# w1's last 96 columns computed beside wqkv's third block, the last rows of the second MLP product packed two token tiles at a time, and the order of work taken from a table

## The chip, the cores and the metric

The kernel runs on one core of one Trainium2 chip. The metric is the device time of one execution in microseconds (us). The kernel before takes 415.14 us (median of three executions, 414.89 to 415.17). The execution that the profiler recorded took 415.18 us, of which 413.4 us lie between its first and its last instruction (the span).

## The reference

For 2048 tokens of 512 numbers, two branches share one layer norm, and the first is gated by the second:

```python
xn = layernorm(x)
# A: sliding, dilated attention: 32 heads of 16, each token sees 8 tokens, two apart
qkv = xn @ wqkv                       # 512 x 1536
o = softmax(q . k[idx] / 4) @ v[idx]  # idx = s, s-2, ..., s-14
s = o @ wo                            # 512 x 512
# B: MLP
h = gelu(layernorm(xn) @ w1 + b1)     # 512 x 1376
m = h @ w2 + b2                       # 1376 x 512
out = x + s * silu(m)
```

## The kernel before

All large products run on PE in float16, each operand split into a high and a low half, so one float32 product is three float16 products (high times high, low times high, high times low).

The tokens are split by parity into two sequences (c = 0, 1) of eight tiles of 128 tokens. The kernel runs eight **attention units** u = (c, hb): each takes one block hb of wqkv (128 columns each of q, k and v, 384 in all). In `qkv` every one of the eight token tiles costs 12 products of 384 columns (L746: four slices of 128 input rows, three half pairs), and ACT or DVE writes the result scaled into U[0] or U[1] (L759, L763). `attention` then runs on DVE: four products and four sums for the logits (L805, L808), the softmax, four products with v (L863, L901 in the last unit), and sums on POOL and DVE. A transposing transfer (L851) brings the result into oT.

The **MLP** goes in four chunks of 512 tokens. 1376 = 10 x 128 + 96, so w1 has eleven column blocks f = 0 to 10, the last of 96 columns. `mlp1` makes, for each f, 12 products of 512 columns into a ps bank (L1016); ACT applies the gelu and makes the high half (L1033, L1036), DVE the low half (L1038). `mlp2` multiplies by block f of w2 two steps later, 12 products of 512 columns into four banks z, one per token tile (L1052). The last block has 97 rows there: 96 and one of ones for b2; its tile is `hlast`. After it ACT applies the silu (L1063, L1068). `wo_first` (L929) and `wo_last` (L961) multiply the attention result by wo, and DVE and POOL combine it with the gate and x.

**Order.** Nothing here is scheduled at run time: every engine works off its instructions in the order written. That order is made while the program is built, by a planner (`Plan`): each operation has an engine, a cost, a priority and the operations it waits for, and the planner always takes the one that can start first, by priority among those. All transfers are issued by SP. PE starts with 24 products of constants (L1169) that keep it working, then takes tokens 6 and 7 of sequence 0 in float32 straight from the loaded data (L617).

In the opening (about 0 to 46 us) x, wqkv and w1 are loaded, normed, split and, for four of the eight tiles, transposed on PE (L683) or by a transfer (L675); units 0 and 1 then run their `qkv`.

Of the kernel before, what the change touches and what calls it, by code (L numbers as in the profile page):

```python
# [33 lines left out]
LASTPOOL = (0, 2, 4)  # L34

# [3 lines left out]
LAG = 2  # L39

# [4 lines left out]
BYDMA = (4, 5, 6, 7)  # L45
TRZ = (3, 3, 0, 2, 0, 1, 1, 0)
PTR = (0.5487, 0.3388, 0.0342, 0.6565, 0.7826, 0.1978, 0.0549, 0.9)
GROUPS = ((0,), (1, 2), (3, 4, 5), (6, 7))
BATCHES = ((0, 1, 2, 3, 4, 5), (6, 7))
LOADS = (('t', 6), ('q', 0), ('q', 2), ('x', 2), ('x', 0), ('q', 4), ('t', 7), ('x', 5), ('x', 1), ('x', 3), ('x', 4), ('q', 6), ('w', 0), ('w', 2), ('x', 7), ('c', 2), ('s', 1), ('c', 0), ('w', 3), ('x', 6), ('w', 1), ('c', 1), ('b', 0), ('s', 0))  # L50
HI_ENG = ('act', 'act', 'act', 'dve', 'dve', 'dve', 'dve', 'act')
XT = (0, 4, 30, 34)
Y_ENG = ('pool', 'act', 'dve', 'dve', 'act', 'pool', 'dve', 'act')

W1ENG = ('act', 'dve', 'act', 'act', 'act', 'act', 'act')
# [3 lines left out]
W2LO = ('dve', 'dve', 'dve', 'dve', 'dve', 'pool', 'dve')  # L59
EV0 = ('act', 'dve', 'dve', 'act', 'act', 'act', 'dve', 'dve')  # L60
EV1 = ('dve', 'dve', 'act', 'act', 'act', 'act', 'dve', 'act')
QLO0 = ('pool', 'dve', 'dve', 'pool')
QLO1 = ('dve', 'dve')
W1LO = ('dve', 'dve', 'pool', 'dve', 'dve', 'dve', 'dve')
WOLAG = 2
MEANBY = ('dve', 'pe', 'pool', 'pool')
W2LATE = 6

BEFORE_W1 = (0, 1, 4, 5)

# [26 lines left out]
class Plan:  # L97
# [9 lines left out]
    def add(self, eng, dur, fn, reads=(), writes=(), prio=None, table=None, nbytes=0,  # L107
            after=None, holds=(), port=False, rate=350e3, issue=0.55, tail=1.4):
# [56 lines left out]
    def start(self):  # L165
        for o in self.ops:
            o.npred, o.ready, o.succs = len(o.preds), 0.0, []
        for o in self.ops:
            for p in o.preds:
                p.succs.append(o)  # L170
        self.free = {o.eng: 0.0 for o in self.ops}
        self.portfree, self.dma, self.landed, self.table = 0.0, 0.0, [], None

    def earliest(self, o):
# [3 lines left out]
        if o.eng == "sp" and o.nbytes:  # L178
            left = FLIGHT
            for end, n in reversed(self.landed):  # L180
                left -= n
                if left < 0:
                    t = max(t, end)
                    break
        return t

    def place(self, o, t):

        if o.eng == "sp":
# [3 lines left out]
            self.dma = max(self.dma, t + o.issue + 0.3)  # L193
            self.dma += o.nbytes / (o.rate if self.dma > SLOW else 265e3)
            end = self.dma + o.tail
            self.landed.append((end, o.nbytes))
            return end
        end = t + o.dur
        if o.nbytes:
            self.free[o.eng] = end  # L200
            self.dma = max(self.dma, end + 0.3) + o.nbytes / o.rate
            return self.dma + o.tail
# [19 lines left out]
    def issue(self):  # L222
# [55 lines left out]
SLOW = 5.5  # L278

FLIGHT = 0.9e6  # L280

PW2 = 1.1284
PS2 = 0.4252
PWQ1 = 0.9
PW1 = 0.423
PB1 = 0.75
PCS = 0.6
PQ0 = 0.2677
PSQ0 = 0.1788
PMEAN = 0.04  # L290
PDIR = (0.192, 0.1517, 0.1187, 0.1556)
PG = (0.5671, 0.5205, 0.3952, 0.4033)
PY = (0.8339, 0.1477, 0.3649, 0.4824, 0.05, 0.5767, 0.05, 0.8333)
PU0 = 0.8687
PU1 = 0.969
PWARM = 0.9
PEV = 0.2698

PTOT = 0.5899

WAKE = 24
PS1 = 1.1561
# [3 lines left out]
PQLO = 0.5225  # L306

PFPLN = 0.35
PSEC = (0.6153, 0.7518, 0.1)

U1MH = 4
# [5 lines left out]
IORD0 = (6, 7, 0, 4, 1, 3, 2, 5)  # L317
IORD1 = (7, 0, 6, 3, 2, 4, 5, 1)
MLPN = (7, 7, 6, 4, 7, 7, 2, 0)
# [7 lines left out]
def tile_mixer(ctx, tc, a_x, a_xt, a_wqkv, a_wo, b_w1, b_b1, b_w2, out):  # L327
# [34 lines left out]
    ident = sb.tile([P, P], F32, name="ident")  # L362
    make_identity(nc, ident)
    fours = sb.tile([P, 2 * P], BF16, name="fours")
    nc.vector.memset(fours, 4.0)
    mean1 = sb.tile([P, P], F32, name="mean1")
    nc.vector.memset(mean1, 1.0 / D)
    halves = sb.tile([P, 16], F32, name="halves")
# [3 lines left out]
    misc = sb.tile([P, 512], F32, name="misc")  # L372
    v0 = misc[64:65]


    wq = sb.tile([P, NHB, 2, KT, 384], F16, name="wq")
    w1 = sb.tile([P, 2, KT * F], F16, name="w1")
# [6 lines left out]
    b1T = sb.tile([P, NF], F32, name="b1T")  # L384
    hlast = sb.tile([P, 2, 512], F16, name="hlast")
# [7 lines left out]
    R_mx = Ring(sb, [P, 64], F32, 4, "mx")  # L393
    R_cs = Ring(sb, [P, NI], F32, 8, "cs")
# [72 lines left out]
    def low_pool(n, lo, get, s, hi, **k):  # L467
# [4 lines left out]
        pool(0.45 + n * 3.9e-3, fn, **k)  # L472
# [25 lines left out]
    def k0(hb):  # L498
        return dict(rate=400e3, tail=0.6, issue=0.45) if hb == 0 else dict(tail=3.5) if hb > 1 else {}
# [9 lines left out]
    def scale_q(hb):  # L509
        col = R_s.new()  # L510
        for k in range(0, KT, 2):
            def go(k=k):
                src = stq[hb]()[:, k * 384:(k + 2) * 384]
                nc.scalar.activation(wq[:, hb, 0, k:k + 2].bitcast(BF16),
# [11 lines left out]
    def prep_q(hb):  # L526
# [3 lines left out]
        for k in range(0, KT, st):  # L530
            n = st * 384
            dst = [wq[:, hb, t, k:k + st].rearrange("p k e -> p (k e)") for t in range(2)]
            src = lambda k=k, n=n: stq[hb]()[:, k * 384:k * 384 + n]
# [17 lines left out]
    def factors(n, V, vs, mk, cdst, ckeys):  # L551
# [12 lines left out]
            rb.t[:, 0:n], p0b.t[:, 0:n], halves[:, 0:n], op=ALU.pow), [p0b], [(rb, 0)], port=False)  # L564
        with pl.fuse():
# [5 lines left out]
            cdst, a1(), halves[:, 8:8 + n], op=ALU.pow), [(A, 1)], ckeys, port=False)  # L571
# [53 lines left out]
    def ln0(g):  # L625
        q, n = cpos[g[0]], len(g)
        for i in g:
# [8 lines left out]
            rb0[:, q:q + n], pb0[:, q:q + n], halves[:, 0:n], op=ALU.pow), [("pb", g)], [("rb", g)], port=False)  # L636

    def second(g):
# [4 lines left out]
        with pl.fuse():  # L643
# [5 lines left out]
            cT[:, 0, q:q + n], x1, halves[:, 8:8 + n], op=ALU.pow), [("ab", g)], [("c", 0, i) for i in g], port=False)  # L649

    def y0(i):
# [12 lines left out]
        elif Y_ENG[i] == "pool":  # L664
            pool(1.25, lambda: nc.gpsimd.tensor_scalar(x(), x(), mv0[:, q, 0:1], rb0[:, q:q + 1], op0=ALU.subtract,
# [701 lines left out]
```

## Time and profile before

| | |
|---|---|
| time, median of three | 415.14 us |
| profiled execution, its time | 415.18 us |
| its span | 413.4 us |
| ACT busy | 222.1 us (54%) |
| POOL busy | 120.3 us (29%) |
| products with wqkv, L746 | 744 |
| first product of the MLP, L1016 | 528 |
| second product of the MLP, L1052 | 528, 48 of them with `hlast` |

A row of the profile gives busy time, the mean of one instruction in ns and the idle time of its engine just ahead. PE products overlap: the recorded length of one product is longer than the distance from one start to the next, and a stream of them costs the distance. In a timeline a row is a group of like instructions, with its start, its length and their count. SPq is the queue in which SP issues transfers.

### The profile page before, as it was taken

How to read it: one execution, taken by the hardware profiler on the slowest of the kernel's cores; microseconds unless marked ns; L12 is line 12 of the kernel's file. 1: busy time of each engine (PE TensorE's matmuls, PEld its weight loads, DVE VectorE, ACT ScalarE, POOL GpSimd, SP SyncE). 2: the span in 40 equal slices, each digit the busy share in tenths (PEclk: the TensorE clock that was granted, in tenths of full speed). 3: DMA queues.
4: the chain of work that ended last, by engine and by line, in shares of the span. 5: the costliest groups of instructions: out<-in, count | busy, mean ns of one | idle time of the engine just before them, and what ended most of it. 6: DMA issues, size and time to landing. Idle time of an engine off the chain costs nothing.

```text
span 413.4 us, 5554 instructions
## 1 busy us (share of the span) xinstructions
PE 405.9 (98%) x2083; PEld 206.6 (50%) x2083; DVE 379.5 (92%) x379; ACT 222.1 (54%) x353; POOL 120.3 (29%) x131
## 2 busy tenths in 40 slices
PE   8799999999999999999999999999999999999996
PEld 5555544445654455445544554455455544444443
DVE  4996989998999999989998999999999998999954
ACT  4699899994549655843384252225212393263500
POOL 3834002004380425042504330434033404520021
PEclk9999999999999999999999999999999999999999
DMA  8958717030045137720172034223604244007133
GB/s 281 397 112 258 235 61 230 0 128 1 1 142 152 28 93 183 149 46 2 48 221 75 0 102 116 68 86 88 205 7 122 88 111 145 0 18 238 23 102 131
DMA packets 47211, 46.41 MB, mean 112 GB/s; under 512 B 31785, under 2 KB 32225, under 8 KB 46673
## 3 DMA queue, kind: packets, MB, share of 16 engines
q1 hardware_dynamic: 47184, 46.06, 37.6%
q8 instruction: 16, 0.26, 0.3%
q14 instruction: 11, 0.08, 0.1%
HBM read 24.06 MB, written 7.34 MB: 76 GB/s over the span
## 4 chain that ended last, share of the span: by engine, by line
PE 92%; ACT 3%; issue 1%; DVE 1%; POOL 1%; ACTq 0%
PE z L1052 28%; PE ps L1016 28%; PE ps L746 25%; PE ps L929 5%; PE ps L961 2%; PE z L961 2%; PE pl L746 1%; ACT w L421 1%; PE pl L961 1%; ACT f L673 1%; ACT yT L687 0%; ACT wq L536 0%; POOL wq L471 0%; POOL rb L635 0%; ACT prod L661 0%
## 5 line engine op out<-in xcount | busy, mean ns | idle before, releaser
L1016 PE MATMUL ps<-yT,w 128*128 128x512 f16 (+1 forms) x528 | 120.4, 379 | 0.0
L746 PE MATMUL ps<-wq,yT 128*128 128x384 f16 x708 | 117.0, 326 | 0.2 <-DVE U L759 0.2
L1052 PE MATMUL z<-w,h 128*128 128x512 f16 x480 | 110.4, 379 | 0.0
L746 PEld LDWEIGHTS <-yT 128*128 128x128 f16 x744 | 72.5, 98 | 49.2 <-issue 1.0
L1016 PEld LDWEIGHTS <-w 128*128 128x128 f16 (+1 forms) x528 | 52.8, 100 | 61.0
L805 DVE TENSOR_TENSOR prod<-U 128x2048 f32<-128x2048 f32 x32 | 73.2, 2286 | 2.2 <-POOL prod L883 0.7
L1052 PEld LDWEIGHTS <-h 128*128 128x128 f16 x480 | 46.6, 98 | 55.5 <-issue 0.3
L808 DVE TENSOR_REDUCE L<-prod 128x128 f32<-128x2048 f32 x32 | 73.0, 2281 | 0.4
L1033 ACT ACTIVATE ps<-ps,b1T,hsc 128x512 f32<-128x512 f32 (+1 forms) x44 | 32.9, 748 | 73.4 <-PE ps L1016 72.2
L863 DVE TENSOR_TENSOR prod<-pl,U 128x2048 f32<-128x2048 f32 x28 | 63.2, 2283 | 4.2 <-POOL prod L873 4.1
L763 ACT ACTIVATE U<-ps,cs 128x384 f32<-128x384 f32 x54 | 31.2, 580 | 65.2 <-PE ps L746 65.2
L873 POOL TENSOR_TENSOR prod<-prod,prod 128x2048 f32<-128x2048 f32 x7 | 31.7, 4531 | 113.8 <-DVE prod L863 99.6
L883 POOL TENSOR_TENSOR prod<-prod 128x1024 f32<-128x1024 f32 x14 | 32.9, 2349 | 0.0
L882 POOL COPY gate<-prod 1x1 f32<-1x1 f32 x21 | 5.5, 264 | 91.0 <-DVE prod L805 82.2
L1038 DVE SCALAR_TENSOR_TENSOR h<-ps,hsc,h 128x512 f16<-128x512 f32 x40 | 29.6, 741 | 1.7 <-ACT h L1036 1.4
L1036 ACT ACTIVATE h<-ps,hsc 128x512 f16<-128x512 f32 x40 | 27.3, 684 | 1.3 <-PE z L1052 0.4
L929 PE MATMUL ps<-wo,oT 128*128 128x512 f16 x96 | 21.7, 379 | 0.0
L858 DVE TENSOR_TENSOR prod<-prod,prod 128x2048 f32<-128x2048 f32 x9 | 20.5, 2282 | 0.0
L1033 ACT ACT_TABLE_LOAD x10 | 12.8, 1283 | 8.6 <-PE ps L1016 8.5
L883 POOL TENSOR_TENSOR prod<-prod,prod 128x1024 f32<-128x1024 f32 x7 | 16.4, 2347 | 0.0
L961 PEld LDWEIGHTS <-oT 128*128 128x128 f16 x108 | 10.6, 98 | 10.4
L929 PEld LDWEIGHTS <-oT 128*128 128x128 f16 x96 | 9.4, 98 | 11.2
(179 smaller groups left out, 377.8 us busy)
## 6 DMA issues: line engine op xcount, KB each, us to landing
f<-in_A_x_dram SPq DMA_DIRECT2D x31, 256.0 KB, 3.5
U<-U SPq DMA_DIRECT2D x16, 392.0 KB, 4.0
gd<-f SPq DMA_DIRECT2D x12, 256.0 KB, 3.4
prod<-in_A_x_dram SPq DMA_DIRECT2D x8, 256.0 KB, 6.9
oT<-in_B_w_dram SPq DMA_DIRECT2D x2, 1024.0 KB
yT<-in_B_w_dram SPq DMA_DIRECT2D x2, 1024.0 KB, 7.9
f<-gd SPq DMA_DIRECT2D x8, 256.0 KB, 2.7
out_dram<-f SPq DMA_DIRECT2D x8, 256.0 KB, 2.8
```

Of the source, the lines that this page charges most:

```text
L746: nc.tensor.matmul(b.t[:, 0:384], y[:, s, k, o:o + P], wq[:, hb, t, k], start=(n == 0), stop=(n == 11))
L763: act(384, lambda i=i, b=b: nc.scalar.activation(U3[:, i:i + 31:15, :], b.t[:, 0:384].rearrange("p (t e) -> p t e", t=3), AF.Identity, sca ...
L805: dve(2048, lambda p2=p2, g=g: nc.vector.tensor_tensor(p2(), q, slots(Ut, KH, 2 * g), op=ALU.mult), qk + [("kh", ub, 0), ("kh", ub, 1), (" ...
L808: dve(2048, lambda pr=pr, g=g: nc.vector.tensor_reduce(L3()[:, 2 * g:2 * g + 2], pr.t.rearrange("p (r f d) -> p r f d", r=2, d=DH), AX.X, ...
L863: dve(2048, lambda: nc.vector.tensor_tensor(pr.t.rearrange("p (r f d) -> p r f d", r=2, d=DH), A3()[:, 2 * g:2 * g + 2].rearrange("p r (f ...
L873: pool(4.75, lambda: nc.gpsimd.tensor_tensor(acc.t, acc.t, p1.t, op=ALU.add), [acc, p1], [acc])
L883: nc.gpsimd.tensor_tensor(x.t[:, 0:1024], x.t[:, 0:1024], y(), op=ALU.add)
L929: nc.tensor.matmul(b.t, oT[:, hb, i // 4, s, i % 4], wo[:, t, hb], start=(hb == 0 and n == 0), stop=(hb == last and n == 2))
L961: nc.tensor.matmul(b.t[:, cols], oT[:, hb, i // 4, s, i % 4], wo[:, t, hb, cols], start=(start and hb == 0 and n == 0), stop=(stop and hb ...
L1016: nc.tensor.matmul(b.t[0:M], w1[:, s, f * 512 + k * M:f * 512 + (k + 1) * M], yT[ch][:, t, k], start=(n == 0), stop=(n == 11))
L1033: act(512, lambda: nc.scalar.activation(b.t[0:M], b.t[0:M], AF.Gelu_apprx_tanh, bias=b1T[0:M, f:f + 1], scale=hsc[0:M, 1:2]), [b, ("b1T",) ...
L1052: nc.tensor.matmul(z.t, hl[s][0:K, t * P:(t + 1) * P], w2[0:K, w, f], start=(f == 0 and n == 0), stop=(f == NF - 1 and n == 2))
```

## The change

**The last 96 columns of w1** are no longer a step of `mlp1`. They lie beside the 384 columns of wqkv's third block (`HLAST = 2`), and `qkv` of that block makes 480 columns per product. The result is now tokens by columns, not columns by tokens. A new function, `last_block`, handles it per chunk of 512 tokens: ACT copies the 96 columns out of the ps bank, POOL adds b1 (loaded as a row on all partitions), ACT applies the gelu and makes the high half, DVE makes the low half in two pieces, and two transposing transfers bring it to columns by tokens.

**The second product** with that block has 3 x 96 + 2 rows to sum. They are packed as two products of 128 rows (96 high rows and 32 low rows each, beside rows of w2 arranged to match) and 34 rows left over. The 34 rows of two token tiles stand on partitions 0 to 33 and 64 to 97 (`hlc`, `w2t`), so the two products of a pair use different rows of the array and different banks. Where there were 12 products per chunk there are now 8 of 128 rows and 4 of 34 rows.

**Around it:** w2 is loaded in two more pieces and split with three more ACT and two more DVE operations; five of seven high halves of w1 are made on DVE (one before); three low halves of w2 are made on POOL (one before); both float32 tiles take their mean from PE; the first row of v goes through DRAM and not through SBUF; other tiles go through the transposing transfer.

**The order** is a table, `ORDER`, with one number per operation. The planner takes the operations in that order and no longer chooses. Its costs for transfers were changed too, but they no longer decide anything.

```diff
+HLAST = 2
-BYDMA = (4, 5, 6, 7)
+BYDMA = (2, 5, 6, 7)
-GROUPS = ((0,), (1, 2), (3, 4, 5), (6, 7))
+GROUPS = ((0,), (1,), (2, 3, 4), (5,), (6, 7))
-W1ENG = ('act', 'dve', 'act', 'act', 'act', 'act', 'act')
+W1ENG = ('dve', 'dve', 'act', 'dve', 'dve', 'act', 'dve')
-MEANBY = ('dve', 'pe', 'pool', 'pool')
+MEANBY = ('pe', 'pe', 'pe', 'dve')
+ORDER = (
+    2, 1, 4, 8, 0, 5, 112, 131, 115, 133, 135, 127, 121, 130, 125, 114, 118, 128, 25, 124, 120, 119, 116, 26,
...
-        order = []
+        order, fixed = [], [self.ops[n] for n in reversed(ORDER)]
         while len(order) < len(self.ops):
             best = None
-            for e, cand in engs.items():
+            if fixed:
+                o = fixed.pop()
...
+                best = (t, o)
+            for e, cand in engs.items() if best is None else ():
...
+    FR = P - FL
+
+    def last_block(ch):
+        n = 4 * FL
+        h16 = R_f.new()
+        v = lambda: h16.t.bitcast(F16).rearrange("p (t a f) -> p t a f", a=2, t=4)
...
+        with prio(PEV):
+            pool(1.0, lambda: nc.gpsimd.tensor_tensor(x3(), x3(), row, op=ALU.add), xk + [("b1T",)], xk)
+            act(n, lambda: nc.scalar.activation(x, x, AF.Gelu_apprx_tanh), xk, xk,
+                aps=1, table="gelu")
+            act(2 * n, lambda: nc.scalar.activation(
+                v()[:, :, :, 0:FL], x.rearrange("p (t o f) -> p t o f", t=4, o=1).to_broadcast([P, 4, 2, FL]),
+                AF.Identity, scale=hsc[:, 2:3]), xk + [("hsc2",)], [(h16, 0)])
...
+            low(lambda: v()[:, :, :, FL:P], 0, 2 * FR, (h16, 1))
+            low(lambda: hrem.rearrange("p a b (o f) -> p (a b) o f", o=2)[:, :, 0:1, 0:FR], 2 * FR, FL, ("hreml",))
...
+            dma(P * 2048, lambda: nc.sync.dma_start_transpose(dst, h16.t.bitcast(F16)), [(h16, k) for k in range(2)] + [("hreml",)],
+                [("hl", ch % 2)], rate=1e6, issue=1.3, tail=0.8)
+            dma(P * 512, lambda: nc.sync.dma_start_transpose(hlc[ch % 2], hrem.rearrange("p a b f -> p (a b f)")),
+                [("hreml",), ("hrem",)], [("hlc", ch % 2)], rate=1e6, issue=1.3, tail=0.8)
...
+        wide = 384 + FL * (hb == HLAST)
...
-                    nc.tensor.matmul(b.t[:, 0:384], y[:, s, k, o:o + P], wq[:, hb, t, k],
+                    nc.tensor.matmul(b.t[:, 0:wide], y[:, s, k, o:o + P], wq[hb][:, t, k],
...
+            if hb == HLAST:
+                act(FL, lambda i=i, b=b: nc.scalar.activation(
+                    hpt[i // 4][:, (i % 4) * FL:(i % 4 + 1) * FL], b.t[:, 384:384 + FL], AF.Identity, scale=hsc[:, 1:2]),
+                    [b, ("hsc",)], [("hp", i // 4, i % 4)], prio=PEV, after=pl.users([("hp", i // 4, i % 4), ("hl", i // 4)]))
+        for j in range(2 if hb == HLAST else 0):
+            last_block(2 * c + j)
...
+        for a in range(0, 4, 2) if f == NF - 1 else ():
+            def pair(a=a, z=list(zt)):
+                ha = hlt[ch % 2].rearrange("p a (t x) -> p (a t) x", t=4)
+                for t in range(a, a + 2):
+                    for w in range(2):
+                        nc.tensor.matmul(z[t].t, ha[:, 2 * t + w], w2[:, w, f], start=False, stop=False)
+                for t in range(a, a + 2):
+                    r = slice(64 * (t - a), 64 * (t - a) + FR + 2)
+                    nc.tensor.matmul(z[t].t, hlc[ch % 2][r, a // 2], w2t[r], start=False, stop=True)
...
-            if p < len(steps):
+            if p < len(steps) and steps[p][1] < NF - 1:
                 with prio(PR_M + p * 10):
                     mlp1(*steps[p])
```

Three places where the order moves. First **SP**, the first loads of the program (U1 takes the float32 tokens and wqkv's second block, prod0 wqkv's first block, prod1 and prod2 the tiles of x). Before:

```order
L1124 DMA U1_87<-in_A_xt_dram 128x512
L505 DMA prod0_93<-in_A_wqkv_dram 128x768 x2
L1099 DMA prod1_94<-in_A_x_dram 128x512 x2
L505 DMA U1_87<-in_A_wqkv_dram 128x768
L1124 DMA U1_87<-in_A_xt_dram 128x512
L1099 DMA prod2_95<-in_A_x_dram 128x512
```

With the change:

```order
L1254 DMA U1_94<-in_A_xt_dram 128x512
L586 DMA prod0_100<-in_A_wqkv_dram 128x768
L1229 DMA prod1_101<-in_A_x_dram 128x512 x2
L1254 DMA U1_94<-in_A_xt_dram 128x512
L1229 DMA prod2_102<-in_A_x_dram 128x512
L586 DMA prod0_100<-in_A_wqkv_dram 128x768
L586 DMA U1_94<-in_A_wqkv_dram 128x768
```

The second half of wqkv's first block moved from third place to seventh, behind three tiles of x and the second float32 tile.

Second **PE**, the second product with the last block, first chunk (z00 to z30 are the banks of the four token tiles; hl0 holds the two packed products, tail the 34 rows). Before, inside the twelve products:

```order
L1052 LDWEIGHTS hlast_91
L1052 MATMUL z00_143<-w2_80,hlast_91 128x512
L1052 LDWEIGHTS hlast_91
L1052 MATMUL z10_144<-w2_80,hlast_91 128x512
L1052 LDWEIGHTS hlast_91
```

With the change:

```order
L1170 LDWEIGHTS hl0_98
L1170 MATMUL z10_148<-w2_87,hl0_98 128x512
L1173 LDWEIGHTS tail_78
L1173 MATMUL z00_147<-tail_78 128x512
L1173 LDWEIGHTS tail_78
L1173 MATMUL z10_148<-tail_78 128x512
L1170 LDWEIGHTS hl0_98
L1170 MATMUL z20_149<-w2_87,hl0_98 128x512
```

Each bank now gets two products of 128 rows, and the 34-row products of two banks follow each other.

Third **ACT**, at the end of unit 2's `qkv` (U0 takes its results; first and hl0 take the 96 columns of chunks 1 and 0). Before:

```order
L1036 ACTIVATE h2_108<-ps2_141,hsc_154 128x512
L763 ACTIVATE U0_86<-ps1_140,cs2_115 128x3x128
L482 ACTIVATE wo_81<-yT2_84,osc_158 128x1024
L763 ACTIVATE U0_86<-ps0_139,cs2_115 128x3x128
L482 ACTIVATE wo_81<-yT2_84,osc_158 128x1024
L763 ACTIVATE U0_86<-ps2_141,cs2_115 128x3x128
```

With the change:

```order
L884 ACTIVATE hl0_98<-ps0_143,hsc_158 128x96
L563 ACTIVATE wo_88<-yT2_91,osc_162 128x1024
L880 ACTIVATE U0_93<-ps1_144,cs2_120 128x3x128
L880 ACTIVATE U0_93<-ps0_143,cs2_120 128x3x128
L880 ACTIVATE U0_93<-ps2_145,cs2_120 128x3x128
L1394 ACTIVATE w2_87<-f6_109,zsc_160 32x512
L884 ACTIVATE first_65<-ps2_145,hsc_158 128x96
L816 ACT_TABLE_LOAD
L816 ACTIVATE hl0_98<-hl0_98 128x384
L818 ACTIVATE f0_103<-hl0_98,hsc_158 128x8x96
```

Between the copy of the last 96 columns and the gelu of chunk 0 stand six operations and a load of ACT's function table; before there was no such chain.

More of the change, by code (lines that the diff above doesn't have):

```diff
@@ L107, in add @@
     def add(self, eng, dur, fn, reads=(), writes=(), prio=None, table=None, nbytes=0,
-            after=None, holds=(), port=False, rate=350e3, issue=0.55, tail=1.4):
+            after=None, holds=(), port=False, rate=390e3, issue=0.45, tail=0.8):
         if self.fused is not None and eng == self.fused["eng"]:
@@ L178, in earliest @@
         if o.eng == "sp" and o.nbytes:
[L179 to L184, printed above, removed]
+            if len(self.landed) >= FLIGHT:
+                t = max(t, self.landed[-FLIGHT])
         return t
@@ L383, in tile_mixer @@
     cT = sb.tile([P, DIL, NI], F32, name="cT")
-    b1T = sb.tile([P, NF], F32, name="b1T")
-    hlast = sb.tile([P, 2, 512], F16, name="hlast")
+    b1T = sb.tile([P, NF + FL], F32, name="b1T")
+    hl0 = sb.tile([P, 512], F32, name="hl0")
+    hpt = [hl0[:, 0:512], first[:, 0:512]]
+    hlt = [h.bitcast(F16).rearrange("p (a t) -> p a t", a=2) for h in hpt]
     gd = dr.tile([DIL, NI, P, D], F32, name="gd")
@@ L854, in emit_o @@
                 [(o16, 0, h0), (o16, 1, h0)], [("oT", hb, h) for h in range(h0, h1)] +
-                ([("s1a", n, 0) for n in range(2)] if u == 0 else []), rate=600e3, issue=1.6)
+                ([("s1a", n, 0) for n in range(2)] if u == 0 else []), rate=1e6, issue=1.3 + 0.7 * (h1 - h0 - 1), tail=0.9)
         def add(n, a, b, d, keys, dkey):
```

268 lines of the change are left out of this document (159 added, 109 removed), and 61 rows, old and new, of the table ORDER.

## The prediction

> **What bounds the kernel now.** I read the busy times of the page first, then its chain of waits, then a table of stretches, then the timeline of the opening and of the end.
>
> ```profile
> PE 405.9 (98%) x2083; PEld 206.6 (50%) x2083; DVE 379.5 (92%) x379; ACT 222.1 (54%) x353; POOL 120.3 (29%) x131
> PE 92%; ACT 3%; issue 1%; DVE 1%; POOL 1%; ACTq 0%
> 0.00:12.00 12.00, 9.82 (x44) 6.12 (x44) 6.31 (x19) 6.11 (x11) 5.24 (x14) 1.00 0.85 298
> 12.00:34.00 22.00, 20.38 (x121) 12.29 (x122) 20.80 (x58) 17.77 (x33) 11.05 (x11) 1.00 0.77 239
> 34.00:389.00 355.00, 354.96 (x1814) 177.82 (x1811) 338.62 (x285) 196.36 (x308) 100.24 (x104) 1.00 0.34 98
> 389.00:410.00 21.00, 20.76 (x109) 10.38 (x106) 13.08 (x19) 1.86 (x3) 3.82 (x3) 1.00 0.36 109
> ```
>
> The stretches give PE, PEld, DVE, ACT, POOL, the granted clock and the transfers. From 34 to 389 us PE stands still for 0.04 us of 355, at full clock, and the chain lies on it for 92% of the span. So a product less on PE is time less, as long as nothing takes PE's place. The candidate is DVE: 338.62 of 355 us busy in the same stretch, with 16.4 us to spare. ACT and POOL have 150 us and more.
>
> **The price of a product** comes from the chain, where a piece is a stretch of PE without a gap.
>
> ```profile
> 101.60 15.60 PE ps L746 x96
> 378.65 2.59 PE ps L1016 x12
> 408.45 1.32 PE ps L961 x12
> L1052 PE MATMUL z<-w,hlast 97*128 97x512 f16 x48 | 11.0, 379 | 0.0
> 378.49 2.75 PE L1016 MATMUL ps<-yT,w 128*96 128x512 f16 x12
> 381.08 5.34 PE L1052 MATMUL z<-w,h 128*128 128x512 f16 x24
> 386.26 2.75 PE L1052 MATMUL z<-w,hlast 97*128 97x512 f16 x12
> 388.85 5.99 PE L961 MATMUL ps<-wo,oT 128*128 128x512 f16 x27
> ```
>
> 384 columns cost 15.60/96 = 0.1625 us, 512 cost 2.59/12 = 0.216, 256 cost 1.32/12 = 0.110. That is a straight line of 0.418 ns per column. Narrowness elsewhere buys nothing: the 96-column block takes from 378.49 to 381.08, 2.59 us, and the 97-row product from 386.26 to 388.85, again 2.59 us.
>
> **The change part by part.** *First product, last block:* 4 chunks x 12 products go: -4 x 2.59 = -10.36 us. They come back as 96 more columns in 2 units x 8 tiles x 12 = 192 products. That is 192 x 96 x 0.418 ns = +7.70 us. Net -2.66.
>
> *Second product, last block:* -4 x 2.59 = -10.36 us again. There come 4 x 8 = 32 products of 128 rows, 32 x 0.216 = +6.91 us, and 8 pairs of 34 rows. No row shows two products on different rows of the array. A pair costs at least one product's distance, 0.216 us, which is 8 x 0.216 = 1.73 in all. At most the two run one after the other, and the array empties ahead of the pair and behind it. What emptying costs is in the row of 48: one product is recorded with 379 ns, a stream costs 216 each, so 163 ns of each lie under the next. Then a pair costs 0.432 + 0.326 = 0.758 us, 6.06 in all. I take 0.30 us, which is 0.216 and half of one emptying, since the pair shares neither array rows nor banks: 8 x 0.30 = +2.40. Net 6.91 + 2.40 - 10.36 = -1.05 (from -1.72 to +2.61).
>
> The page TensorEngine Tiling (Array Packing) of the Trainium skill, section Key Properties, speaks against the change here: going over to another tiling mode drains TensorE. By it each pair has two drains, and with 163 ns for one and full overlap between, eight pairs cost 8 x 0.54 = 4.3 us. The second product would then come out 0.9 us dearer than before. The page TensorE: Matmul & The Clock Gate of the Trainium skill, section on packing small matmuls, has tiles start about 4 ns apart. By it alone eight pairs cost 1.8 us. No trace here has yet shown either.
>
> *Opening.* Here the table changes nearly every row, so I walked it with durations of before.
>
> ```profile
> 6.84 0.84 ACT L514 ACTIVATE wq<-prod 128x768 bf16<-128x768 f32 x1 [1.41 <-DMA prod<-in_A_wqkv_dram]
> 8.92 2.13 ACT L536 ACTIVATE wq<-prod,qsc 128x384 f16<-128x384 f32 x4 [1.15 <-DVE qsc L459]
> 9.83 0.97 PEld L599 LDWEIGHTS ps<-U,mean 128*128 128x128 f32 x8 [0.40 <-DMA U<-in_A_xt_dram]
> 15.96 0.81 PE L746 MATMUL ps<-wq,yT 128*128 128x384 f16 x4
> 19.54 4.71 PE L746 MATMUL ps<-wq,yT 128*128 128x384 f16 x28
> 24.44 5.36 PE L746 MATMUL ps<-wq,yT 128*128 128x384 f16 x32 [0.19 <-DVE U L759]
> 41.19 5.20 PE ps L746 x32
> 46.38 10.36 PE ps L1016 x48
> ```
>
> Before, 8 + 28 = 36 products of units 0 and 1 are done by 24.44 us; the other 132 need 132 x 0.1625 = 21.45 us and end at 46.38, so 0.5 us is lost there. Now wqkv's second half of block 0 is the seventh load, with 2048 KB through it. Before, 2176 KB had landed at 9.83, so it lands near 9.5 and not near 6.84 us. ACT then has 14.5 us of rows in series (four squares, four scalings of 0.53 and two of 0.92, four tiles to norm, four casts) ahead of the high half of block 1, which is ready between 23.4 and 24.1 us. PE's order has 36 products of block 0 ahead of it, from about 16.2 us; they end near 23. So PE enters block 1 0.3 to 1.0 us sooner, and loses perhaps the 0.5 us elsewhere. I take -0.6 us. A walk over some forty rows may miss by 2 us each way: -2.5 to +1.5.
>
> *The new chain to the second product* has one narrow place, chunk 0. Its order on PE after unit 2's last product has 36 products of w1 and 12 of w2, 48 x 0.216 = 10.4 us, and then reads the transposed block.
>
> ```profile
> L763 ACT ACTIVATE U<-ps,cs 128x384 f32<-128x384 f32 x54 | 31.2, 580 | 65.2 <-PE ps L746 65.2
> L536 ACT ACTIVATE wq<-yT,qsc 128x768 f16<-128x768 f32 x4 | 3.6, 921 | 0.0
> L1033 ACT ACT_TABLE_LOAD x10 | 12.8, 1283 | 8.6 <-PE ps L1016 8.5
> L863 DVE TENSOR_TENSOR prod<-pl,U 128x2048 f32<-128x2048 f32 x28 | 63.2, 2283 | 4.2 <-POOL prod L873 4.1
> 370.05 2.09 SPq L851 DMA_TRANSPOSE oT<-o  x1
> ```
>
> ACT's last write of the unit (0.58), a w2 scaling (0.7), a copy (0.3), the table load (1.28), the gelu (0.6) and the high half of 768 (0.92) end 4.5 us after the unit. DVE's two small low halves (0.7 together) and the transfer (2.1) make it 7.3. But two products with v of 2.28 stand ahead on DVE, and the second low half and the 34 rows of w2 (three more DVE operations) follow. So it is 9 to 12 us against 10.4. I take +0.3 us (0 to 1.5). The other three chunks have a whole unit or several steps as cover.
>
> *Costed at nothing:* 16 copies, 4 gelus and 4 high halves on ACT (some 11 us, against 9 that go with the block's eight and four high halves of w1), POOL's bias adds and w2 halves (POOL is idle 293 us), two more loads and eight transposes on SP. DVE loses and gains about as much: four low halves of 0.74, the mean of one tile and three halves of weights go, eight small low halves, w1's high halves and two w2 operations come. I make it +0.7 us. All this is hidden by PE's stream, and costs its length if DVE falls behind.
>
> ```profile
> 389.58 0.74 DVE L848 SCALAR_TENSOR_TENSOR o<-prod,osc,o 128x512 f16<-128x512 f32 x1
> 390.34 4.67 SPq L851 DMA_TRANSPOSE oT<-o  x2
> 392.97 0.75 DVE L848 SCALAR_TENSOR_TENSOR o<-prod,osc,o 128x512 f16<-128x512 f32 x1 [0.79 <-ACT o L846]
> 396.62 2.10 PE L961 MATMUL ps<-wo,oT 128*128 128x512 f16 x9
> ```
>
> *The end* shows the cover. The attention's first half is written at 390.3 us and landed 2.1 us later, 392.4; PE asks for it at 396.6, 13.2 us before its last product ends at 409.8. The change puts nine products of other tiles ahead of that, so that PE asks 39 x 0.216 + 24 x 0.11 = 11.1 us before its end. With PE ending 4 us sooner, near 405.7, it asks at 394.6: DVE may come 2.2 us later than before, and 0.7 uses a third of that.
>
> **Sum:** -2.66 - 1.05 - 0.6 + 0.3 = -4.0 us on the profiled 415.18 us (span 413.4 and 1.78 around it), so 411.2. The median of three is 0.04 lower: 411.1 us.
>
> **The rivals.** (a) *Every pair drains the array twice.* 0.54 instead of 0.30 us makes eight pairs 1.9 us dearer, the rest as forecast: 413.0 us. For it: 163 ns do lie under each product. Against: nothing in the trace changes shape, so nothing shows the price. The tiling page of the Trainium skill, cited above, is this rival's rule.
>
> (b) *DVE takes PE's place, at the last attention unit.* The first attention now starts later, since DVE makes four more high halves of w1 ahead of it: 2944 columns at 0.49 us for 512 (row below) are 2.8 us. If DVE keeps its 12 idle us of the middle and adds this, its first half is written more than 2.2 us later and each further us costs one. Slower than before by 0.2% needs 4.0 + 2.2 + 0.8 = 7 us of delay: 416.5 us. For it: DVE has only 16.4 us of slack in 355. Against: it stood idle 3 us between 36 and 40 us, which the earlier work now fills. A smaller delay, 1.5 to 3 us beyond the cover, gives 412.6 to 414.1.
>
> ```profile
> 32.19 0.49 DVE L480 TENSOR_SCALAR w<-oT,hsc 128x512 f16<-128x512 f32 x1
> 36.00:38.00 2.00, 2.00 (x14) 1.22 (x13) 0.34 (x3) 1.97 (x4) 1.97 (x1) 1.00 0.58 210
> 38.00:40.00 2.00, 2.00 (x14) 1.21 (x13) 0.66 (x2) 2.00 (x5) 1.58 (x1) 1.00 0.82 240
> ```
>
> (c) *The table gains more.* Pairs fully side by side (-0.7 more) and a stream that enters block 1 2 us sooner: 408.8 us. For it: PE's idle time, 3.8 us ahead of 34 us, is all in the opening. Against: the walk, where ACT holds block 1 to 23.4 or later.
>
> (d) *The change does not do what it says:* 480 columns cost a whole bank's 0.216 us. Then 192 x 0.0535 = 10.3 us come back and not 7.7: 413.8 us. Against: 256, 384 and 512 lie on one line.
>
> **Chances.** Forecast 0.50 (its own range 409.6 to 412.4), (a) 0.15, (b) 0.17, of which 0.09 slower than before, (c) 0.13, (d) 0.05. A measurement of this kernel tells about 0.2%, 0.83 us, from no change. Faster than 414.3 us are the forecast, (a), (c), most of (d) and the small case of (b): 0.86. Within 0.2% I give 0.05, slower 0.09. The range reaches to (c) below and past (a) and (d) above: 408.7 to 414.0 us.
>
> **What would show it.** Right: groups of 480 columns with 96 in 19.4 us; no row of 96 columns by 512; the 34-row products in starts a few ns apart; PE without gaps after the opening; the first product of the MLP's second stage with the packed block without a wait. Wrong: gaps of over 0.1 us around the 34-row products (a); PE waiting for oT in the last 15 us (b); PE waiting for the transposed block or for DVE after unit 2; more or less than 36 products of wqkv done at 24 us (opening).

## The result, and the profile after

The changed kernel takes **429.74 us** (median of four executions, 427.39 to 430.08) against 415.01 us for the kernel before beside it: 1.0343 times as long, with a 95% interval of 1.0306 to 1.0381. The forecast was 411.1 us, 408.7 to 414.0. It was wrong in sign. The profiled execution took 430.0 us, with a span of 428.2.

The page of the changed kernel answers to the lines shown of before: busy times, the chain of waits by engine, and the granted clock in 40 slices.

```profile
PE 408.4 (95%) x2041; PEld 200.9 (47%) x2041; DVE 391.8 (91%) x388; ACT 223.3 (52%) x372; POOL 128.8 (30%) x139
PE 74%; DVE 10%; issue 5%; DMA 3%; POOL 2%; ACT 2%; SPq 1%; DVEq 0%; POOLq 0%; ACTq 0%
PEclk9999999999998999999999999999999999989998
```

PE has 42 products fewer and is busy 2.5 us longer. It stands idle for 19.8 us of the span, where it stood 7.5 before, and the chain lies on it for 74% and no longer for 92%. The clock, which was full all through, dips.

The view of what PE waits for names the places (time in total, times, longest):

```profile
PE z L1170 <- DMA hl<-f: 3.4, 1, 3.4
PE ps L1052 <- DVE f L1066: 2.5, 1, 2.5
PE ps L1139 <- DVE h L1157: 2.0, 1, 2.0
PE z L516 <- ACT w L1364: 1.6, 1, 1.6
```

None of these waits was there before. The timeline of PE shows what follows the first three; the start is in front, the wait in brackets:

```profile
131.58 1.86 PE L1170 MATMUL z<-w,hl 128*128 128x512 f16 x4 [3.40 <-DMA hl<-f]
308.79 4.44 PE L1052 MATMUL ps<-wo,oT 128*128 128x512 f16 x12 [2.45 <-DVE f L1066]
377.04 4.44 PE L1139 MATMUL ps<-yT,w 128*128 128x512 f16 x12 [2.00 <-DVE h L1157]
```

Twelve products take 4.44 us here and 2.59 elsewhere; four take 1.86 and not 0.86. The table of stretches shows why (PE, PEld, DVE, ACT, POOL, clock, transfers):

```profile
308.00:310.00 2.00, 1.21 (x4) 0.53 (x4) 2.00 (x4) 0.07 (x1) 1.89 (x2) 0.75 0.00 0
310.00:312.00 2.00, 2.00 (x7) 0.62 (x5) 1.97 (x2) 0.45 (x1) 0.00 (x0) 0.50 0.00 0
312.00:314.00 2.00, 2.00 (x10) 0.90 (x9) 2.00 (x2) 0.24 (x1) 0.00 (x0) 0.89 0.00 0
```

The granted clock falls to one half about when PE starts again, and stays there for 3.4 us: the three stretches lack 0.25, 0.50 and 0.11 of 2 us each, 1.72 us in all.

**Who is late.** DVE's busy time rose from 379.5 to 391.8 us. The timelines of DVE and POOL show four rows with most of it; here are three, with POOL's rows beside them:

```profile
122.44 4.00 DVE L825 SCALAR_TENSOR_TENSOR hrem<-hl,hsc,f 128x128 f16<-128x128 f32 x1 [1.09 <-ACT f L818]
302.97 5.11 DVE L928 TENSOR_TENSOR prod<-U 128x2048 f32<-128x2048 f32 x1 [1.70 <-ACT h L1155]
350.49 6.24 DVE L928 TENSOR_TENSOR prod<-U 128x2048 f32<-128x2048 f32 x1
121.77 4.53 POOL L996 TENSOR_TENSOR prod<-prod,prod 128x2048 f32<-128x2048 f32 x1
301.42 4.51 POOL L996 TENSOR_TENSOR prod<-prod,prod 128x2048 f32<-128x2048 f32 x1 [12.49 <-DVE prod L986]
305.89 3.05 POOL L815 TENSOR_TENSOR first<-first,b1T 128x384 f32<-128x384 f32 x1
350.06 4.51 POOL L996 TENSOR_TENSOR prod<-prod,prod 128x2048 f32<-128x2048 f32 x1 [11.26 <-DVE prod L986]
```

The same operations take 0.34 and 2.28 us elsewhere. POOL's adds end at 126.30, 305.93 and 354.57; DVE's rows end 0.14, 2.15 and 2.16 us later. So DVE stood until POOL's add was over and then did its own work at the usual speed. At 305.89 POOL's next add, 1.00 us elsewhere, waits in its turn until DVE is done. The section Who interferes with whom of the Trainium skill's page SBUF — State Buffer has this rule: a DVE instruction with two SBUF inputs and a GpSimd instruction that reads SBUF use one shared port, and whoever comes first holds it for the whole instruction. The trace agrees to 0.2 us.

**The end** is later too: the last output pieces are written by DVE at 421.54, and the span ends 6.7 us later. Before, the same distance was 2.7 us. SP's queue and DVE's last row:

```profile
420.79 0.75 DVE L1123 TENSOR_TENSOR U<-U 128x256 f32<-128x256 f32 x2
422.92 0.46 SPq L1046 DMA_DIRECT2D out_dram<-f  x1
423.43 1.43 SPq L1125 DMA_DIRECT2D out_dram<-U  x3
```

The two narrow pieces, finished last, stand fourth and sixth of ten on that queue. The four issues shown, and one between, carry pieces that were ready before the two narrow ones were.

**The account**, from 413.4 to 428.2 us. PE's work: -3.1 (402.8 us in experiment 5, whose profiled execution keeps full clock while PE has work, against 405.9) and +5.6 for half clock. PE's idle time: three waits +7.85, the wait at 52 us with the 0.3 behind it +1.9, the end +4.2 (7.8 us after PE's last product, 3.6 before), the opening -1.7. The sum is +14.75, and +14.8 was measured.

### The profile page after: what moved, and what is told of

Read it like the earlier page. It is cut to its first block, busy times and chain, and to the rows that moved or that the text cites. A ratio compares the mean times of both kernels' runs of the same rounds, so it can differ in the third digit from the quotient of the medians.

```text
span 428.2 us, 5508 instructions
## 1 busy us (share of the span) xinstructions
PE 408.4 (95%) x2041; PEld 200.9 (47%) x2041; DVE 391.8 (91%) x388; ACT 223.3 (52%) x372; POOL 128.8 (30%) x139
## 4 chain that ended last, share of the span: by engine, by line
PE 74%; DVE 10%; issue 5%; DMA 3%; POOL 2%; ACT 2%; SPq 1%; DVEq 0%; POOLq 0%; ACTq 0%
PE ps L862 25%; PE ps L1139 19%; PE z L1182 18%; PE ps L1052 5%; DVE prod L928 3%; PE ps L1084 2%; PE z L1084 2%; DVE L L931 2%; PE z L1170 2%; DMA prod<-in_A_wqkv_dram 1%; DVE prod L986 1%; DVE prod L981 1%; DVE h L1157 1%; DVE hrem L825 1%; PE pl L862 1%
## 5 line engine op out<-in xcount | busy, mean ns | idle before, releaser
L862 PE MATMUL ps<-wq,yT 128*128 128x384 f16 (+1 forms) x720 | 129.2, 337 | 0.0
L1139 PE MATMUL ps<-yT,w 128*128 128x512 f16 x480 | 110.5, 383 | 2.3 <-DVE h L1157 2.0
L1182 PE MATMUL z<-w,h 128*128 128x512 f16 x480 | 111.7, 379 | 0.1
L928 DVE TENSOR_TENSOR prod<-U 128x2048 f32<-128x2048 f32 x32 | 79.9, 2499 | 5.4 <-DMA U<-U 2.5
L1139 PEld LDWEIGHTS <-w 128*128 128x128 f16 x480 | 47.0, 99 | 61.2 <-issue 7.4
L1152 ACT ACTIVATE ps<-ps,b1T,hsc 128x512 f32<-128x512 f32 x40 | 29.7, 746 | 36.9 <-PE ps L1139 36.7
L1005 POOL COPY gate<-prod 1x1 f32<-1x1 f32 x21 | 4.2, 202 | 128.8 <-DVE prod L928 113.6
L1155 ACT ACTIVATE h<-ps,hsc 128x512 f16<-128x512 f32 x40 | 27.0, 683 | 12.7 <-PE z L1182 12.3
L1052 PE MATMUL ps<-wo,oT 128*128 128x512 f16 x96 | 23.4, 400 | 2.5 <-DVE f L1066 2.5
L969 ACT ACTIVATE o<-prod,osc 128x1024 f16<-128x1024 f32 (+1 forms) x9 | 9.5, 1052 | 22.9 <-DVE prod L981 12.2
L1052 PEld LDWEIGHTS <-oT 128*128 128x128 f16 x96 | 9.8, 102 | 15.2 <-issue 4.9
```

What stands on the lines that cost most here:

```text
L862: nc.tensor.matmul(b.t[:, 0:wide], y[:, s, k, o:o + P], wq[hb][:, t, k], start=(n == 0), stop=(n == 11))
L928: dve(2048, lambda p2=p2, g=g: nc.vector.tensor_tensor(p2(), q, slots(Ut, KH, 2 * g), op=ALU.mult), qk + [("kh", ub, 0), ("kh", ub, 1), (" ...
L1052: nc.tensor.matmul(b.t, oT[:, hb, i // 4, s, i % 4], wo[:, t, hb], start=(hb == 0 and n == 0), stop=(hb == last and n == 2))
L1139: nc.tensor.matmul(b.t[0:M], w1[:, s, f * 512 + k * M:f * 512 + (k + 1) * M], yT[ch][:, t, k], start=(n == 0), stop=(n == 11))
L1152: act(512, lambda: nc.scalar.activation(b.t[0:M], b.t[0:M], AF.Gelu_apprx_tanh, bias=b1T[0:M, f:f + 1], scale=hsc[0:M, 1:2]), [b, ("b1T",) ...
L1182: nc.tensor.matmul(z.t, hl[s][:, t * P:(t + 1) * P], w2[:, w, f], start=(f == 0 and n == 0), stop=False)
```

## The experiments

Every kernel has line numbers of its own, so one operation has other numbers in the lines of other runs.

Theory A: the loss is that DVE and POOL shut each other out at three places where PE's cover is thin. The order table puts DVE's operation ahead of POOL's add at 303 and 350 us, and 22 DVE operations between its operands and it at 122 us, but nothing on the chip makes POOL wait for them. In the table, 1071 is the q-k product of 303 us and 955 is POOL's add:

```
954, 953, 1071, 878, 955, 919, 912
```

On the chip DVE reached 1071 late, POOL had its operands, and took the port. What DVE waited for were the transfers that bring the neighbouring rows of K (U<-U): the row above names ACT, on which 1071 does not depend, and the rows of experiments 5 and 7 at this place name the transfer. Rivals: B, DVE has too much work in any case; C, the clock falls by itself.

**1. POOL's add held back at the three places** (e1_pin).

```diff
+ PIN = (1, 5, 6)
...
+ ahead.setdefault(u, pr)
...
- pool(4.75, lambda: nc.gpsimd.tensor_tensor(acc.t, acc.t, p1.t, op=ALU.add), [acc, p1], [acc])
+ def first_add():
+     if u in PIN:
+         nc.gpsimd.tensor_copy(gate, ahead[u + 1].t[0:1, 0:1])
+     nc.gpsimd.tensor_tensor(acc.t, acc.t, p1.t, op=ALU.add)
+ pool(4.75, first_add, [acc, p1], [acc])
```

> The changed kernel with one addition: GpSimd's first 4.5 us add of the attention units 1, 5 and 6 (L996) waits until the next unit's first q-k product is written, which is where the order table has it; a 1x1 copy of that product stands ahead of the add. Nothing else moves. Theory A (the two engines exclude each other: a DVE operation that reads two operands from SBUF stands until GpSimd's add beside it ends, at 122, 303 and 350 us): the DVE rows of 4.00, 5.11 and 6.24 us go back to 0.34, 2.28 and 2.28, DVE's busy time falls by about 10 us to 381-382, PE's waits of 3.4, 2.5 and 2.0 us go, and with them the slow products behind them (2.6 + 1.9 + 1.9 us). Sum -14 us: about 416 us, from 414.5 to 418.5, with the granted clock at 1.00. Theory B (DVE simply has too much work in this order, the stretched rows are a symptom): DVE's busy time falls but PE waits for DVE elsewhere, 424 us or more. Theory C (the clock falls by itself, not from the waits): the clock stays near 0.984 and the time is 421 to 424 us. The waits at 52 us and the late end stay under each.

Measured: **417.88 us** (417.49 to 420.10), 11.9 us less than the changed kernel, from three 1x1 copies. DVE's busy time fell to 381.2 us, PE's to 403.2, and the three waits are gone; what PE still waits for:

```profile
PE z L517 <- ACT w L1369: 1.9, 1, 1.9
PE z L1306 <- DVE first L439: 1.2, 1, 1.2
PE ps L863 <- DVE f L1071: 1.0, 1, 1.0
```

A holds; B and C fall. The gain is 2 us under the 14 expected: a wait of 1.0 us came where DVE is still late at 308 us. The mean clock was 0.989 to 0.995 and not the 1.00 expected. In the profiled execution that costs nothing: its clock is full up to 412 us, and PE's last product ends at 408.3.

**2. The narrow output pieces last on SP's queue** (e2_tail): in the table 1263 and 1259 move to the end.

> The changed kernel with one change in the table: the two narrow output transfers (256 columns) stand last on SP's queue, and not fourth and sixth of ten. Theory A (the queue's order: five finished pieces wait behind the two last ones, at about 0.48 us of issue each): the end comes 2.4 to 4 us sooner, 2.7 us after DVE's last operation as before the change; 427.0 us, from 425.8 to 427.8 if the rest of the run repeats 429.7. Theory B (the transfers are bound by how fast they land): within 0.5 us of the changed kernel.

Measured: 426.20 us (425.15 to 429.18), 3.5 us less. The end comes 3.7 us after DVE's last operation, and not 6.7. The queue's order it was; 1 us against before stays.

**3. The planner's rules in place of the table** (e3_free).

```diff
- ORDER = (
...
- )
+ ORDER = ()
```

> The changed kernel without its order table: the planner's own rules set the order, with all other constants of the change, so the new computation (480 columns, pairs of 34 rows, new chain) is the same, and the order another. Theory A (the loss is the table's): the rules give the port to whoever is ready first, so no DVE operation is stretched by more than about 2.4 us and PE's three waits with slow clock are not there as such; 409 to 419 us, with the products of 480 columns and the pairs at the same 0.2025 and 0.32 us. Theory B (the new computation itself, its longer chain and DVE's work, costs the time): 424 us or more.

Measured: 429.42 us (427.57 to 430.27). Both theories' signs appear. No DVE row of 128x2048 or of the low halves is stretched, and DVE's busy time is 381.1 us, as A has it. But the time is B's. PE's timeline says where it went:

```profile
60.57 4.19 PE L1076 MATMUL ps<-yT,w 128*128 128x512 f16 x12 [2.92 <-DVE h L1094]
133.40 7.93 PE L1076 MATMUL ps<-yT,w 128*128 128x512 f16 x36
146.90 1.44 PE L1107 MATMUL z<-w,hl 128*128 128x512 f16 x3 [5.56 <-ACT f L602]
143.02 1.23 SPq L768 DMA_TRANSPOSE hl<-f  x1
```

The transposed block of chunk 0 is issued at 143.02 and is wanted at 141.3. (The row names ACT's L602, which ends at that moment; the products read the block and nothing that L602 writes.) The chain from unit 2's last product is 13.5 us long here, and 36 products of cover are 7.8. In this order the new computation gains nothing. The table keeps this chain shorter and puts 48 products ahead of the packed block.

**4. Edits 1 and 2 together** (e4_both).

> The two edits together: the three adds wait as in the table, and the two narrow output pieces go out last. Theory A: the two gains add up, -14 and -2.7 us: about 413.2 us, from 411.5 to 416. Theory B (DVE's amount of work): 421 us or more. Theory C (clock by itself): 418 to 421 us.

Measured: 415.35 us (median of nine executions, 413.34 to 417.56; a tenth took 419.63), a ratio of 1.0011 to before (0.9984 to 1.0038): no difference. The two gains add to 14.4 us where 16.5 was expected. What is left against the forecast are PE's waits at 53 us (1.56 and 0.30) and near 301 and 309 us (0.26 and 1.47), and an end that is 1.3 us longer than before. The hand-over at chunk 0 now fits, with next to nothing to spare:

```profile
117.34 7.93 PE L1141 MATMUL ps<-yT,w 128*128 128x512 f16 x36
125.11 2.75 PE L1184 MATMUL z<-w,h 128*128 128x512 f16 x12
127.70 1.03 PE L1172 MATMUL z<-w,hl 128*128 128x512 f16 x4
124.33 1.27 SPq L829 DMA_TRANSPOSE hl<-f  x1
```

**5. One hold taken back, unit 5** (e5_one: `PIN = (1, 6)`).

> The kernel with both edits, with one taken back: in attention unit 5 GpSimd's first add again starts as soon as its operands are there (units 1 and 6 still wait). Theory A (a wait of PE of 2 us and more also costs clock): the 5.1 us row of DVE at about 303 us is back, PE waits 2.4 us for L1066's operation (1.5 us there with both edits) and its next 12 products take 4.4 instead of 2.6 us: 415.7 + 0.9 + 1.9 = 418.5 us, from 417.3 to 420, the granted clock at about 0.99. Theory C (the clock falls by itself): the 12 products behind that wait take 2.6 us and the time is 416 to 417 us.

Measured: 417.34 us (416.50 to 417.89). The wait came back to the hundredth, the slow products did not. PE, DVE and POOL at that place:

```profile
302.38 2.75 PE L1054 MATMUL ps<-wo,oT 128*128 128x512 f16 x12 [2.45 <-DVE f L1068]
297.15 4.51 DVE L926 TENSOR_TENSOR prod<-U 128x2048 f32<-128x2048 f32 x1 [2.30 <-DMA U<-U]
299.47 3.05 POOL L813 TENSOR_TENSOR first<-first,b1T 128x384 f32<-128x384 f32 x1
```

A wait of 2.45 us, and twelve products at full speed behind it: theory A as to the clock (every wait of 2 us and more costs clock) falls. The median lies at the lower edge of theory A's range and above theory C's; the time alone decides nothing. The clocks of the four executions were 0.999, 0.993, 0.999 and 1.000.

**6. One hold taken back, unit 1** (e10_first: `PIN = (5, 6)`), the place that the prediction priced at 0.3 us.

> The kernel with both edits, with one taken back: in attention unit 1 GpSimd's first add again starts as soon as its operands are there (units 5 and 6 still wait). This is the place of the hand-over to the second product at chunk 0. Theory A (the hand-over is late only because DVE's 128x128 low half stands behind that add): the 4.00 us row is back, the transposed block comes 3.3 us after PE asks for it, and there is nothing of it elsewhere; 415.7 + 3.3 = 419.0 us where the clock holds and about 421 where a half-clock stretch follows, 418.5 to 421.5. Theory F (the new chain to the second product is too long in itself, the add only one of its causes): PE waits for the transposed block with the add held back too, and taking the hold away adds less than 2 us, 417.5 us or less.

Measured: 420.57 us (418.67 to 422.69). The wait is back with 3.3 us and the two low halves `hrem<-hl` again take 3282 ns in the mean. F falls: with the add held back PE does not wait here at all. In the profiled execution half clock follows this wait, and also the wait of 1.89 us at 53 us. The execution with the clock at 0.999 took 418.67 us, the three at 0.989 to 0.992 took 419.86 to 422.69.

**7. The add in four pieces, nothing held back** (e8_split).

```diff
- pool(4.75, lambda: nc.gpsimd.tensor_tensor(acc.t, acc.t, p1.t, op=ALU.add), [acc, p1], [acc])
+ def first_add():
+     for c0 in range(0, 2048, 512):
+         d = acc.t[:, c0:c0 + 512]
+         nc.gpsimd.tensor_tensor(d, d, p1.t[:, c0:c0 + 512], op=ALU.add)
+ pool(4.75, first_add, [acc, p1], [acc])
```

> The changed kernel with GpSimd's first add of every unit (128x2048, 4.5 us) written as four adds of 512 columns (1.27 us each by the row L1120), nothing held back and the table as it is. Theory A (an operation waits until the other engine's running instruction ends, and gets in between two of them): DVE's rows of 4.00, 5.11 and 6.24 us fall to at most 1.7, 3.6 and 3.6, PE's waits of 3.4, 2.5 and 2.0 us fall to under 1 us, and their slow products go; 418 us, from 416 to 421. Theory D (GpSimd keeps its turn through a run of its own instructions): the rows stay at 4 us and more, 429 to 432 us.

Measured: 419.17 us (417.54 to 420.77), 10.6 us less than the changed kernel. DVE's row at 303 us went from 5.11 to 3.16, and PE's wait of 3.4 us to 1.5, where less than 1 was expected:

```profile
297.73 3.16 DVE L928 TENSOR_TENSOR prod<-U 128x2048 f32<-128x2048 f32 x1 [1.62 <-DMA U<-U]
```

So DVE gets in between two of POOL's instructions, and D falls. A wait is as long as what is left of one instruction of the other engine.

**8. The kernel before without its gates** (e6_nogate): the copies of L882 are taken out.

> The kernel before, without the 1x1 copies (L882) that hold each of GpSimd's 2.35 us half adds back until a q-k product is written; the adds then start when their operands are there, beside whatever DVE does. Theory A (DVE's operations on two SBUF operands and GpSimd's adds exclude each other): rows of DVE longer than 2.9 us where before all of 128x2048 took 2.28, DVE's busy time 5 to 25 us above 379.5, and the time 416.5 to 428 us. Theory B (they share the memory without harm): DVE's busy time within 1 us of 379.5 and 415 us.

Measured: 415.14 us (415.04 to 416.62) against 414.74, ratio 1.0014 (1.0004 to 1.0023). The mechanism is there, its price is not (L882 is POOL's add in this kernel, since the copy's line is gone):

```profile
L805 DVE TENSOR_TENSOR prod<-U 128x2048 f32<-128x2048 f32 x32 | 79.3, 2477 | 1.3 <-POOL prod L882 0.6 <-DMA U<-U 0.3
PE 405.5 (98%) x2083; PEld 206.5 (50%) x2083; DVE 384.3 (93%) x379; ACT 222.2 (54%) x353; POOL 136.8 (33%) x110
```

The expected time was missed. This group lost 6.1 us, in pieces of up to 1.7 (its longest row is 3.99), DVE 4.8 in all, and PE waited for next to none of it. What a stretched row costs is decided by the cover at its place.

**9. A forced wait in the kernel before** (e9_wait3, e9_wait5, e9_wait8, with 3, 5 and 8 more writes), for the clock.

```diff
- act(512, lambda: nc.scalar.activation(hi()[0:M], b.t[0:M], AF.Identity,
-                                       scale=hsc[0:M, 2:3]), [b], [hk])
+ def high():
+     for _ in range(1 + 8 * ((ch, f) == (2, 2))):
+         nc.scalar.activation(hi()[0:M], b.t[0:M], AF.Identity, scale=hsc[0:M, 2:3])
+ act(512, high, [b], [hk])
```

> The kernel before, with one forced wait and nothing else: for one step of the MLP (third chunk, hidden block 2, at about 219 us) ScalarE writes the same high half three times more, at 0.66 us each, and PE asks for it 0.2 us after it is ready. PE should wait 1.8 us there. Theory A (the clock falls when PE stands still, whatever its length above 1 us): half clock behind it in each run, clock under 0.997 and 414.8 + 1.8 + 1.9 = 418.5 us. Theory E (the clock is judged over stretches of some us that begin at any time; a wait shorter than one seldom empties it): the clock stays at 0.999 to 1.000 in most runs, 416.6 us.

> As the run with three, with five more writes: PE waits 3.1 us. Theory A: half clock in each run, 419.8 us. Theory E: half clock in some runs and not in others, so two groups of times about 2 us apart, 417.9 and 419.8 us. Theory C (the clock has nothing to do with waits): 417.9 us at a clock of 1.000 in every run.

> As the run with three, with eight more writes: PE waits 5.1 us. Theories A and E: half clock behind it in every run, 414.8 + 5.1 + 2 = 421.9 us, clock about 0.995. Theory C: 419.9 us at a clock of 1.000.

Measured: 414.92, 415.25 and 418.99 us. The expected waits were wrong: PE does not read this half at 220 us, and the cover hid the first two almost whole (no wait, and 0.3 us). Only eight writes made one, of a length that is known from above:

```profile
233.96 2.40 PE L746 MATMUL ps<-wq,yT 128*128 128x384 f16 x7 [2.45 <-DVE h L1040]
```

Its four executions took 419.35, 418.85 and 419.13 us at a clock of 0.996, and 417.92 at 1.000. The same program loses clock in three executions of four, and that costs 1.2 us. One of the four was profiled; that the others had the same wait is likely and not shown.

What decides is where the wait lies, and the traces show it. The half clock always lasts 3.41 us, or twice that (behind the wait of 5.56 us in experiment 3). In the changed kernel, read in stretches of 0.1 us, it begins at 131.51, 309.01 and 377.27 us, and the distances are 52 and 20 times 3.413 us. So there is a grid of windows of 3.41 us. PE was busy for 0.07, 0.97 and 1.42 us of the windows just ahead. In experiment 5 the wait of 2.45 us fell across two windows with 1.81 and 2.57 us of work, and the clock stayed full. Over the twelve profiled executions in which the grid can be placed, each window with up to 1.44 us of work is followed by half clock. No window with 1.81 us or more at full clock is. In between (1.56, 1.72 and 1.77 us) one of three is. The Trainium skill's page TensorE: Matmul & The Clock Gate, in its Part 1, has windows of 3.4 us that run free of the program, and these runs agree with that. It has the clock fall after an idle window; here windows with up to 1.44 us of work were enough.

**10. Five rows of the table moved, on top of edits 1 and 2** (e7_move): 231 goes ahead of 270 and 516 ahead of 249 (the wait at 53 us), 926 and 927 ahead of 875 (the transfers of K's neighbouring rows), 886 behind 1245 (an output row).

> The kernel with both edits, and six rows of the table moved: at 53 us one eviction of q and k goes ahead of the square sums of w2 on ScalarE and twelve products of w1 ahead of the column sum on PE; at 290 us the transfers of K's neighbours go ahead of three loads on SP; one finished output row goes out earlier. Theory A (what is left are waits that single rows of the order make): PE's wait of 1.6 us at 53 us goes, that of 1.5 us at 309 falls to under 0.8, the end comes about 0.5 us sooner: 415.7 - 1.6 - 0.9 - 0.5 = 412.7 us, from 410.8 to 414.2, under the kernel before. Theory B (DVE's amount of work): the waits come back elsewhere, 415 to 417 us.

Measured: **414.04 us** (412.78 to 415.16, nine executions), 0.9979 times the time before (0.9966 to 0.9993). It is the only version that beats the kernel before, by 0.2%. PE's wait at 308 us is gone; that at 53 us moved rather than went:

```profile
PE ps L1141 <- DVE h L1159: 1.6, 1, 1.6
PE ps L1141 <- ACT U L878: 0.4, 1, 0.4
```

The square sums of w2 need weights that have only just landed, and whichever operation is put ahead, the next one is behind them.

## Why the prediction was wrong

**Right: the price of the stream.** The chain of the changed kernel has the new products without a gap, behind the entry into block 1 that is used below:

```profile
16.13 1.49 PE ps L862 x8
18.73 3.90 PE ps L862 x24
22.74 5.85 PE ps L862 x36
209.14 0.86 PE z L1170 x4
210.00 0.32 PE z L1173 x2
273.14 14.58 PE ps L862 x72
```

480 columns cost 14.58/72 = 0.2025 us, so 192 products cost 192 x 0.040 = 7.7 us more, as forecast; rival (d) falls. Four products of 128 rows take 0.86 us, that is 0.216 each, and a pair of 34-row products takes 0.32 us. The forecast was 0.30 and rival (a) 0.54, so (a) falls. The page TensorEngine Tiling (Array Packing) of the Trainium skill has, under Key Properties, a drain of TensorE at each change of the tiling mode; at the 163 ns of the row of before, two of them would have made the pair 0.54, and the trace has 0.32. The second product is then -10.36 + 6.91 + 8 x 0.32 = -0.89 us, and both together -3.55; PE's busy time fell by 3.1.

**Right in sign, larger than taken, and given back: the opening.** PE enters block 1 at 22.74 us, 1.7 sooner than before; -0.6 was taken, with bounds of -2.5 to +1.5. At 52 us it loses 1.9 us, because the square sums of w2 wait for their weights. The walk stopped before that place.

**Wrong: the chain at chunk 0, +0.3 us (0 to 1.5).** It cost 3.3 to 3.4 us of waiting in the three profiled executions that have the whole add and no hold, each with a stretch of half clock behind it. The length of the chain was right: 10.4 us of cover, and without the clash the block is there when PE asks (experiment 4). The failed term is "DVE's two small low halves (0.7 together)": one of them took 4.00 us. All its durations came from rows of DVE alone.

**Wrong, and the main failure: "costed at nothing".** "POOL is idle 293 us" and "all this is hidden by PE's stream" treat POOL as a separate resource. The prediction did say that the work costs its length if DVE falls behind, but it looked for that in DVE's own work alone. DVE's busy time was forecast at +0.7 and measured at +12.3 us. Four stretched rows make it: 4.00 - 0.34, 5.11 - 2.28, 6.24 - 2.28 and one of 2.58 - 0.34 are 12.7 us. The first three reach PE. With the clock behind them they are worth the 11.9 us that experiment 1 gave back. The walk took the moved rows at places where a term was seen, and not each of POOL's adds against the DVE operations that the new table puts beside it.

The trace of before had shown it. Two rows of DVE there (L713 and L920) are twice as long as the others of their kind (0.68 us), each under an add of POOL:

```profile
140.32 1.52 DVE L713 TENSOR_TENSOR f<-f,f 128x512 f16<-128x512 f32 x1
137.46 2.28 DVE L863 TENSOR_TENSOR prod<-pl,U 128x2048 f32<-128x2048 f32 x1
136.74 4.55 POOL L873 TENSOR_TENSOR prod<-prod,prod 128x2048 f32<-128x2048 f32 x1 [14.00 <-DVE prod L863]
261.74 1.82 DVE L920 TENSOR_TENSOR f<-f,f 128x512 f32<-128x512 f32 x1
258.48 4.54 POOL L873 TENSOR_TENSOR prod<-prod,prod 128x2048 f32<-128x2048 f32 x1 [15.02 <-DVE prod L863]
```

POOL's add ends at 141.29 and 263.02, DVE's rows 0.55 and 0.54 us later. The product of L863, one input of which lies in PSUM (pl), runs inside the first add at its usual 2.28 us, so the clash is with two inputs in SBUF, as in the rule cited above. A mean (810 and 824 ns in the groups) hides this; the longest of a group shows it. The program of before says it too: its planner marks operations of DVE and POOL with `port` and starts none of them before `portfree`, so the order that it makes, and the table, are free of the clash only as long as the chip keeps the planner's times.

**Wrong: the end.** The cover for the last attention was kept: PE never waits for oT, so rival (b) did not come at its place. Its engine was the right one, its mechanism not. Of the 4.2 us at the end, 3.0 are the order of the output transfers (6.7 against 3.7 us, experiment 2), which the prediction did not look at; the cause of the rest stays open.

**The chances.** Slower had 0.09, and all of it on one mechanism. Rivals (a), (c) and (d) moved a price by 1.9 to 2.7 us, and (b) was 416.5 us, where its own 7 us of delay make 415.9; none asked what a new order for every row does when the chip runs a little otherwise than the table's model.

**What stays open.** The 5.6 us of half clock in the profiled execution depend on how each wait falls on the windows of 3.41 us (experiment 9), and the forecast had no term for it. Where the grid begins differs from execution to execution; the runs don't show what sets it. Whether an order found anew, with the holds in it, reaches the -4 us was not tried.

## What to carry to other kernels

A fixed order across engines is only kept where a semaphore keeps it. Where a table or a planner's model serializes two engines on a shared resource, the chip gives it to whoever arrives first; three 1x1 copies that make the later one wait took 0.17 us of POOL each and gave back 11.9.

Before an engine is called idle, look at the longest row of each group beside its median, and at what the other engines did in that time. A busy engine's added work can hide; a 4 us instruction on an idle one can stop it.

## What was not expected of the hardware

Two DVE operations of 0.34 us took 4.00 and 2.58 us beside POOL's adds. A wait of 2.0 us cost 1.9 us more than its length, through half clock (4.44 for 2.59 us of products), and one of 2.45 us passed without it, since it fell across two windows of 3.41 us. Two products of 34 rows on different rows of the array take 0.32 us together, where one of 128 rows takes 0.216.
